# A kept clock that books VectorE's steps longer beside GpSimd, one kind of step per fill, and the last network's transposes in other banks

## The chip, the cores and the metric

The kernel runs on one core of a Trainium2 chip. The metric is the device time of one execution in microseconds, the median of three runs.

## What is computed

Three layers follow one another on 1152 tokens (2 batches of 576) of width 512: attention over a window of 128 with 8 heads and a linear bias; a network of four experts which all run and are weighted by normalised probabilities; and a last network with a squared relu, whose hidden width 2048 the kernel treats as two more experts.

```
x   = window attention(q, k, v)                 # 8 heads of 64
p   = probs / sum(probs)
x   = sum over e of p[e] * (relu(x @ w1[e]) @ w2[e])     # 512 -> 1024 -> 512, e = 0..3
out = square(relu(x @ w_in)) @ w_out                     # 512 -> 2048 -> 512
```

## The kernel before

All matmuls take float32 operands in two rounded parts, high and low, and add three products (high by high, high by low, low by high). The rounding of a weight is two kinds of step: ScalarE copies the tile to its rounded part and GpSimd subtracts for the rest (`rest`, L489).

A planner orders the attention and expert 0 (about the first 143 us). Behind it stands a loop over `items`. An item of one kind is a first matmul group of 384 tokens and one 128-wide tile of hidden units, followed by its second group (`gemm1`, L925, and `gemm2`, L1149). An item of the other kind, a pair (`gemm1_pair`, L1039, and `gemm2_pair`, L1114), computes a two by two block product with seven products instead of eight; its operands are sums: of weight blocks (`w_forms`, made by GpSimd at L345, rounded by ScalarE at L369, rests by GpSimd into `ls`) and of blocks of x (`x_forms`, VectorE at L961, ScalarE at L992). Experts 1 (its second half), 2, 3 and the second half of the last network (e = 5) run as pairs; expert 0, the first half of expert 1 and e = 4 don't. The first pair starts near 226 us, e = 4 runs from 479 to 577, e = 5 behind it. Within a pair three banks `pa`, `pb`, `pc` hold the products: `p1` copies the first one (ScalarE, L1050), `u2` adds it to the second (VectorE, L1054), and the fifth product accumulates on the bank that `u2` has read; `u3` does the same for the seventh. For e = 5 the squared relu of the first block goes by ScalarE (L1068), a VectorE product (L1069) and a copy to `hmem` (L1070). The second group's results gather in banks of kind "y" and VectorE adds them into SBUF (L1164 to L1176).

The weights of the last network come as float64 and are made into float32 from their two 32-bit words, in 32 units (`convert`, L223): a load, ScalarE's `begin` (L268), on VectorE a clamp (L275), a shift (L278) and two joins (L285), then a store from ScalarE's queue (L251). They are read again later by SyncE's queue.

What runs between the matmul groups is set by `fill(share, us, need)`. It moves a kept clock on by the booked length of the matmuls just issued (`clock["now"]`) and then issues background steps: a step of `xbg` (sums of x) on every other call, up to three steps of conversion if `need` is above 0 and credit is there, then weight steps `bg` by quota. The kept clock also holds the booked end of each engine's queue (`spent`); `room` and `by` let a step pass when an engine or an earlier result is near enough, `spare` when VectorE would still be done within `need`. If weights are not ready when an item needs them, `want` issues all that is missing ahead of the item. All engines run their instructions in the order of issue.

The transposed tiles of x for the last network (`to_x2`) come in while expert 3 ends and in the first items of e = 4; they take a bank of kind "work", of which there are three, shared with `hps`. There are five banks of kind "y".

Of the kernel before, what the change touches and what calls it, by code (L numbers as in the profile page):

```python
# [130 lines left out]
def kernel(  # L131
# [91 lines left out]
    def convert():  # L223
# [10 lines left out]
        def load(j, eng):  # L234
            i, h = todo[j]
            src, nk, nf = w_src(*order[i])
            raw[j] = places[j % 2][0]
            m = nk // 2
            eng.dma_start(
                out=raw[j].rearrange("p (k f) t -> p k (f t)", k=m).bitcast(mybir.dt.int64),  # L240
                in_=src[:, h * m:(h + 1) * m, :],
            )
            at["raw", j] = clock["now"] + 6.0

# [13 lines left out]
        def steps(j):  # L258
            a = both[:, j % 2, :]
            ai = a.bitcast(I32)  # L260

            def begin():
                if not (by(at["raw", j]) and by(at.get(("gone", j - 2), 0.0))):
                    return False
                if not room("ACT", 1.2):
                    return False
                hi = raw[j][:, :, 1]
                nc.scalar.activation(out=a, in_=hi.bitcast(F32), func=ACTF.Abs, scale=65536.0)  # L268
                at["a", j] = spent("ACT", 0.7)

            def shift():
                if not (by(at["a", j]) and spare(1.1)):
                    return False
                spent("DVE", 1.1)
                nc.vector.tensor_scalar(  # L275
                    out=a, in0=a, scalar1=8053063680.0, scalar2=2.0, op0=ALU.min, op1=ALU.max
                )
                nc.vector.tensor_scalar(  # L278
                    out=ai, in0=ai, scalar1=3, scalar2=None, op0=ALU.logical_shift_left
                )  # L280

            def join(part, amount, op):
                if not spare(0.8):
                    return False
                nc.vector.scalar_tensor_tensor(  # L285
                    out=ai, in0=raw[j][:, :, part], scalar=amount, in1=ai, op0=op,
                    op1=ALU.bitwise_or,
                )
                at["out", j] = spent("DVE", 0.8) + 0.5

            ops = [
                begin, shift, lambda: join(1, -(1 << 31), ALU.bitwise_and),
                lambda: join(0, 29, ALU.logical_shift_right),
            ]
            if j:
                ops.insert(1, lambda: swap(j - 1))
            if j + 1 == len(todo):
                ops += [lambda: swap(j), lambda: (fxkeep.append(places[0]), fxkeep.append(places[1]),
                                                  free.append(buf))[-1]]
            return ops  # L300
# [17 lines left out]
    def spare(us):  # L318

        now = clock["now"]  # L320
        return clock["force"] or max(clock["DVE"], now) + us <= now + clock["need"]

    def by(end):

        return clock["force"] or end <= clock["now"] + 0.5

    def w_forms(i):
# [14 lines left out]
        def add(o, x, y, op):  # L342
            if not room("POOL"):
                return False
            nc.gpsimd.tensor_tensor(out=t["s"][:, o:o + 2, :], in0=x(), in1=y(), op=op)  # L345
            t["end"] = spent("POOL", 0.75)

# [10 lines left out]
        def part_lo(o, src):  # L358
            if not room("POOL"):
                return False  # L360
            js = slice(o, o + 2)
            rest("POOL", t["la"][0][:, js, :], src, t["ha"][0][:, js, :])
            spent("POOL", 0.75)

        def round_s(o):
            if not (by(t["end"]) and room("ACT", 1.2)):
                return False
            js = slice(o, o + 4)
            nc.scalar.activation(out=t["hs"][0][:, js, :], in_=t["s"][:, js, :], func=ACTF.Copy)  # L369
            t["hs", o] = spent("ACT", 0.6)  # L370

        def done(o):
# [6 lines left out]
            rest("POOL", t["ls"][0][:, js, :], t["s"][:, js, :], t["hs"][0][:, js, :])  # L379
            spent("POOL", 0.75)  # L380
            if o == 6:
# [18 lines left out]
    def w_ops(i):  # L400
# [24 lines left out]
        def lo(o):  # L425
# [3 lines left out]
            rest("POOL", flat(held[0][1])[:, cs], raw[:, cs], flat(held[0][0])[:, cs])  # L429
            spent("POOL", 0.75)  # L430
            if o == 2 * n - 2 * P:
# [519 lines left out]
    def x_forms(ch, eng):  # L951
# [14 lines left out]
        def make(i, name, terms):  # L966
# [12 lines left out]
            def total(k):  # L979
# [4 lines left out]
                else:  # L984
                    z, o = more[k - 1]
                    op(place(i), place(i), f32(z), o)
                end["sum"] = spent("DVE", 0.9)

# [6 lines left out]
            def lo():  # L995
                if not room("DVE"):
                    return False
                op(f[name][1], place(i), f32(f[name][0]))
                spent("DVE", 0.9)

# [26 lines left out]
    def gemm1_pair(e, ch, g):  # L1027
# [29 lines left out]
        def relu(i, j, src, place=None):  # L1057
            hh, hl = (x[:, j * n:(j + 1) * n] for x in h[i])
            spent("DVE", 0.2 + 0.0013 * n, step)
            spent("ACT", 0.1 + 0.0009 * n, step)  # L1060
# [30 lines left out]
        mm(pa, a12, f["b21"], False, True)  # L1091
        relu(0, 0, pa, c22)
        mm(pb, s3, f["t3"], False, False)
        add(u3, pb, p1)
        fill(0.6, step)
        mm(pc, s4, f["b22"], False, True)
# [7 lines left out]
        relu(1, 1, c22)  # L1104
        fill(0.6, step, 1.5 + 1.4 * (2 * n // P))
        return h
# [73 lines left out]

    def to_x2(nt):
        tp = ps_tile("work", [P, KT, P], "xtp")
        for k in range(KT):
            nc.tensor.transpose(
                out=tp[:, k, :], in_=ytile[nt][:, k * P:(k + 1) * P], identity=ident
            )
        ns = slice(nt * P, (nt + 1) * P)
        nc.scalar.activation(out=xh[:, :, ns], in_=tp, func=ACTF.Copy)
        nc.vector.tensor_tensor(out=xl[:, :, ns], in0=tp, in1=f32(xh[:, :, ns]), op=ALU.subtract)  # L1189
# [49 lines left out]

    def run_x2(n=1):  # L1240
        for _ in range(min(n, len(x2todo))):
            to_x2(x2todo.pop(0))

    def flush_one():
# [9 lines left out]
        for tile_ in ys[e, ch]:  # L1254
# [4 lines left out]
            if last:  # L1259
                evac(e, ch, [tile_], f, two)  # L1260
            elif two:
                run_x2()
            i = len(ys[e, ch]) - 1 - tile_[0]
            need = 1.5 + (1.38 - 0.74 * last) * i if two else 3.0 + 0.69 * i
            fill(0.5 if two and last else 1.0, 1.38 if two else 0.69, need)
# [47 lines left out]
    def fill(share, us, need=0.0):  # L1313
# [4 lines left out]
        if xbg and (x_turn[0] % 2 or x_late):  # L1318
            if xbg[0]() is not False:
                xbg.pop(0)  # L1320
        conv_due[0] = min(conv_due[0] + RATE * us, 6.0)
        for _ in range(3):
            if conv and need and conv_due[0] >= 1.0 and conv[0]() is not False:
                conv_due[0] -= 1.0
                conv.pop(0)
        quota["left"] += quota["n"] * share / quota["per"]
        while quota["left"] >= 1.0:
            if not bg_some(1):
# [316 lines left out]
    fxwork, fxbuf, fxkeep, x_late, conv = [], [], [], [], []  # L1645
    conv_due, RATE = [0.0], 0.6

# [7 lines left out]
    xbg = x0_most + x1_most + x0_last + x1_last  # L1655
    xbg.append(lambda: (free.extend(fxbuf), fxbuf.clear()))
    x_turn = [0]

# [14 lines left out]
    for it, (e, ch, f, two) in list(enumerate(items))[N1:]:  # L1673
# [8 lines left out]
        if e >= E and (ch or f):  # L1682
            run_x2()
        quota["n"] = pace(it)
        if two:
            while xbg and (ch or e > E and len(xbg) > x_rest[0]):
                clock["force"] = True
# [69 lines left out]
```

## Time and profile before

| | us |
|---|---|
| median of 3 runs | 687.25 |
| lowest and highest | 686.38, 688.24 |
| the profiled execution | 685.12 |
| its span, first to last instruction | 683.3 |

Busy share of that span: TensorE 97%, VectorE 69%, GpSimd 55%, ScalarE 45%. The granted clock of TensorE was 0.99 over the span. Times in the rows below are microseconds from the span's start. A group names a source line, an engine and the tile written, "<-" the tiles read; a bracket gives the idle time of the engine before the instruction and who ended it.

### The profile page before, as it was taken

Reading aid. Unit: us, or ns where it says so; the run is one execution under the profiler, and the core shown is the slowest. Engines: PE = TensorE matmul, PEld = TensorE weight load, DVE = VectorE, ACT = ScalarE, POOL = GpSimd, SP = SyncE. Lnnn points to the kernel's source line nnn. Section 1 sums busy time; section 2 is a strip of 40 time slices with the busy share of each in tenths; the row PEclk is TensorE's granted clock in tenths of the full one; section 3 lists DMA queues with packets and bytes.
Section 4 is the critical chain, followed back from the end, with each engine's and each line's share of the span. In section 5 each row is a group of like instructions: output and inputs, shape, how many; then the busy total and the mean of one; then the engine's idle time right before and its main releaser. Section 6 shows DMA issues by size and latency. Waiting matters only on the chain.

```text
span 683.3 us, 10748 instructions
## 1 busy us (share of the span) xinstructions
PE 664.7 (97%) x3840; PEld 590.6 (86%) x3840; DVE 472.3 (69%) x958; ACT 308.6 (45%) x745; POOL 378.1 (55%) x459
## 2 busy tenths in 40 slices
PE   8999999999999989999999999999999999899997
PEld 7778888889999878898888989898899899799896
DVE  4798898844768887878878877877458543644453
ACT  5798787623323433434334443433455443423220
POOL 3799995527600954735645644242458974864321
PEclk8999999999999999999999999999999999999999
DMA  8943222013423342443343525343101011000012
GB/s 211 276 110 93 66 78 57 11 63 112 165 80 105 108 155 92 154 129 117 115 151 108 170 78 183 125 154 109 61 2 67 26 62 31 2 0 1 1 63 77
DMA packets 44022, 64.42 MB, mean 94 GB/s; under 512 B 4160, under 2 KB 26176, under 8 KB 43968
## 3 DMA queue, kind: packets, MB, share of 16 engines
q1 hardware_dynamic: 33248, 39.61, 19.3%
q10 hardware_dynamic: 10720, 24.12, 10.5%
q8 instruction: 30, 0.49, 0.3%
q14 instruction: 24, 0.20, 0.1%
HBM read 52.97 MB, written 10.75 MB: 93 GB/s over the span
## 4 chain that ended last, share of the span: by engine, by line
PE 70%; POOL 10%; DVE 9%; issue 6%; ACT 2%; SPq 1%; DMA 1%; POOLq 0%; ACTq 0%
PE yacc L1114 21%; PE hps L1039 20%; PE hps L925 11%; PE yacc L1149 10%; POOL wl L489 4%; PE xps L720 3%; POOL hmem L489 2%; PE tp L848 2%; DVE wconv L285 2%; DVE hmem L1075 2%; DVE y L1168 2%; PE sc L800 1%; POOL wsum L345 1%; DMA rk<-in_kT_dram 1%; DVE c L1054 1%
## 5 line engine op out<-in xcount | busy, mean ns | idle before, releaser
L1114 PE MATMUL yacc<-wh,hmem 128*128 128x512 f32 x504 | 160.8, 391 | 0.0
L489 POOL TENSOR_TENSOR wl<-wraw,wh 128x256 fp32r<-128x256 f32 (+1 forms) x118 | 108.6, 946 | 77.6 <-ACT wh L422 52.9
L1149 PE MATMUL yacc<-wh,hmem 128*128 128x512 f32 x344 | 112.0, 393 | 0.4 <-POOL hmem L489 0.4
L1114 PEld LDWEIGHTS yacc<-wh,hmem 128*128 128x128 f32 x504 | 94.7, 188 | 19.1
L1114 PE MATMUL yacc<-wl,hmem 128*128 128x512 f32 x252 | 98.4, 390 | 0.0
L925 PE MATMUL hps<-xh,wh 128*128 128x384 f32 (+1 forms) x256 | 83.2, 325 | 0.6 <-DVE xl L1189 0.6
L925 PE MATMUL hps<-xh,wl 128*128 128x384 f32 (+1 forms) x256 | 81.6, 319 | 0.0
L925 PE MATMUL hps<-xl,wh 128*128 128x384 f32 (+1 forms) x256 | 81.5, 318 | 0.0
L1149 PEld LDWEIGHTS yacc<-wh,hmem 128*128 128x128 f32 x344 | 64.5, 188 | 13.9 <-POOL hmem L489 0.8
L1149 PE MATMUL yacc<-wl,hmem 128*128 128x512 f32 x172 | 67.3, 391 | 0.0
L489 POOL TENSOR_TENSOR ls<-wsum,hs 128x256 fp32r<-128x256 f32 x56 | 48.2, 884 | 31.2 <-ACT hs L369 30.5
L1050 ACT ACTIVATE p<-hps 128x256 f32<-128x256 f32 (+1 forms) x56 | 22.7, 408 | 77.7 <-PE hps L1039 63.8
L285 DVE SCALAR_TENSOR_TENSOR wconv<-wraw,wconv 128x512 int32<-128x512 int32 x64 | 56.4, 881 | 1.8
L345 POOL TENSOR_TENSOR wsum<-wraw 128x256 f32<-128x256 f32 x28 | 24.1, 862 | 56.6 <-PE hps L925 35.5
L1114 PEld LDWEIGHTS yacc<-wl,hmem 128*128 128x128 f32 x252 | 47.4, 188 | 8.8
L836 POOL TENSOR_SCALAR ts<-ts,st 128x256 f32<-128x256 f32 (+2 forms) x80 | 40.6, 521 | 25.7 <-DVE st L831 12.1
L1074 ACT ACTIVATE hmem<-c 128x256 fp32r<-128x256 f32 (+1 forms) x60 | 26.1, 445 | 56.7 <-DVE c L1054 55.9
L489 POOL TENSOR_TENSOR hmem<-c,hmem 128x256 fp32r<-128x256 f32 (+1 forms) x32 | 27.1, 856 | 43.3 <-ACT hmem L1070 29.0
L925 PEld LDWEIGHTS hps<-xh,wh 128*128 128x128 f32 x256 | 48.2, 188 | 2.0 <-DVE xl L1189 1.0
L925 PEld LDWEIGHTS hps<-xl,wh 128*128 128x128 f32 x256 | 48.3, 189 | 0.7 <-issue 0.2
L489 POOL TENSOR_TENSOR hmem<-r,hmem 128x384 fp32r<-128x384 f32 x24 | 26.0, 1086 | 40.2 <-ACT hmem L1136 40.1
L925 PEld LDWEIGHTS hps<-xh,wl 128*128 128x128 f32 x256 | 48.2, 188 | 0.0
(141 smaller groups left out, 1670.6 us busy)
## 6 DMA issues: line engine op xcount, KB each, us to landing
wraw<-in_w_dram SPq DMA_DIRECT2D x32, 512.0 KB, 4.6
w<-wconv ACTq DMA_DIRECT2D x32, 256.0 KB, 2.4
wraw<-in_w_out_dram ACTq DMA_DIRECT2D x16, 512.0 KB, 3.9
wraw<-w SPq DMA_DIRECT2D x16, 512.0 KB, 4.0
wraw<-in_w_in_dram ACTq DMA_DIRECT2D x14, 512.0 KB, 3.8
rq<-in_qT_dram SPq DMA_DIRECT2D x8, 256.0 KB, 7.1
out_dram<-y SPq DMA_DIRECT2D x8, 256.0 KB, 2.0
rk<-in_kT_dram SPq DMA_DIRECT2D x8, 192.0 KB, 5.9
```

The source lines that it names most:

```text
L285: nc.vector.scalar_tensor_tensor(out=ai, in0=raw[j][:, :, part], scalar=amount, in1=ai, op0=op, op1=ALU.bitwise_or,)
L345: nc.gpsimd.tensor_tensor(out=t["s"][:, o:o + 2, :], in0=x(), in1=y(), op=op)
L489: e.tensor_tensor(out=out, in0=in0, in1=f32(in1), op=ALU.subtract)
L720: nc.tensor.matmul(out=xps[:, :, o0:o0 + w], lhsT=l_, rhs=r_, start=(i == 0 and l_ is wh_ and r_ is hi), stop=(i == len(mm) - 1 and l_ is ...
L836: nc.gpsimd.tensor_scalar(out=ts[0:n, g, :], in0=ts[0:n, g, :], scalar1=st[0:n, 2, g:g + 1], scalar2=1.0, op0=ALU.mult, op1=ALU.mult,)
L848: nc.tensor.transpose(out=tp[0:cn, g, k * n:(k + 1) * n], in_=s["ts"].tile[0:n, g, c0:c0 + cn], identity=ident[0:n, 0:n],)
L925: nc.tensor.matmul(out=ps, lhsT=l_[:, k, cs], rhs=r_[:, k, cols], start=(k == 0 and r_ is xh and l_ is wh and not second), stop=(k == KT - ...
L1039: nc.tensor.matmul(out=ps, lhsT=a[l_][:, k, :], rhs=b[r_][:, k, :], start=start and k == 0 and l_ == r_, stop=stop and k == 1 and l_ == 1, ...
L1050: nc.scalar.activation(out=out, in_=x, func=ACTF.Copy)
L1074: nc.scalar.activation(out=hh, in_=src, func=ACTF.Relu)
L1114: nc.tensor.matmul(out=y, lhsT=l_[:, ns], rhs=r_[:, fo, :], start=(first and fo == 0 and j == 0), stop=(last and fo == FTQ - 1 and j == 2),)
L1149: nc.tensor.matmul(out=y, lhsT=l_[:, ns], rhs=r_[:, fo, :], start=(first and j == 0), stop=(last and j == 2),)
```

## The change

The kept clock: a VectorE step asked for by `spare` is booked at 1.6 times its length while GpSimd's booked end lies ahead, at 1.1 times else, and `spare` books it itself. Clamp and shift become two steps at 0.45 (one at 1.1 before), a join costs 0.65 (0.8). GpSimd's steps cost 0.85 (0.75), the sums of x 0.2 + 0.003 n (0.9). `by` takes how early a step may pass, and for two of them it is 0. The windows `need` behind a pair's first group and its output tiles start from 0.8 (1.5). `fill` issues no weight step in a call that issued a conversion step; the credit of conversion is capped at 12 (6). In the last network the first relu of a pair is issued behind `u3`, and the transposes of e = 4 take banks of kind "y" and are booked. The sums of x that a first pair needs are forced ahead of it for every expert.

```diff
-            at["raw", j] = clock["now"] + 6.0
+            at["raw", j] = clock["now"] + 7.0
...
-            def shift():
-                if not (by(at["a", j]) and spare(1.1)):
+            def clamp():
+                if not (by(at["a", j], 0.0) and spare(0.45)):
                     return False
-                spent("DVE", 1.1)
                 nc.vector.tensor_scalar(
                     out=a, in0=a, scalar1=8053063680.0, scalar2=2.0, op0=ALU.min, op1=ALU.max
                 )
+
+            def shift():
+                if not spare(0.45):
+                    return False
                 nc.vector.tensor_scalar(
                     out=ai, in0=ai, scalar1=3, scalar2=None, op0=ALU.logical_shift_left
                 )
             def join(part, amount, op):
-                if not spare(0.8):
+                if not spare(0.65):
                     return False
...
-                at["out", j] = spent("DVE", 0.8) + 0.5
+                at["out", j] = clock["DVE"] + 0.5
...
     def spare(us):
         now = clock["now"]
-        return clock["force"] or max(clock["DVE"], now) + us <= now + clock["need"]
-    def by(end):
-        return clock["force"] or end <= clock["now"] + 0.5
+        us *= 1.6 if clock["POOL"] > now + 0.2 else 1.1
+        if not clock["force"] and max(clock["DVE"], now) + us > now + clock["need"]:
+            return False
+        return spent("DVE", us)
+    def by(end, early=0.5):
+        return clock["force"] or end <= clock["now"] + early
...
         def round_s(o):
-            if not (by(t["end"]) and room("ACT", 1.2)):
+            if not (by(t["end"], 0.0) and room("ACT", 1.2)):
...
     def gemm1_pair(e, ch, g):
...
         mm(pa, a12, f["b21"], False, True)
-        relu(0, 0, pa, c22)
+        if e < E:
+            relu(0, 0, pa)
         mm(pb, s3, f["t3"], False, False)
         add(u3, pb, p1)
+        if e >= E:
+            relu(0, 0, pa, c22)
...
-        fill(0.6, step, 1.5 + 1.4 * (2 * n // P))
+        fill(0.6, step, 0.8 + 1.4 * (2 * n // P))
...
-    def to_x2(nt):
-        tp = ps_tile("work", [P, KT, P], "xtp")
+    def to_x2(nt, kind):
+        tp = ps_tile(kind, [P, KT, P], "xtp")
...
+        spent("ACT", 0.6)
+        spent("DVE", 0.7)
...
-            need = 1.5 + (1.38 - 0.74 * last) * i if two else 3.0 + 0.69 * i
+            need = 0.8 + (1.38 - 0.74 * last) * i if two else 3.0 + 0.69 * i
...
-        conv_due[0] = min(conv_due[0] + RATE * us, 6.0)
+        conv_due[0] = min(conv_due[0] + 0.6 * us, 12.0)
+        given = False
         for _ in range(3):
             if conv and need and conv_due[0] >= 1.0 and conv[0]() is not False:
                 conv_due[0] -= 1.0
                 conv.pop(0)
+                given = True
         quota["left"] += quota["n"] * share / quota["per"]
-        while quota["left"] >= 1.0:
+        while quota["left"] >= 1.0 and not given:
...
+    x_rest = [len(x1_last) + 1]
...
         if e >= E and (ch or f):
-            run_x2()
+            run_x2("y")
         quota["n"] = pace(it)
         if two:
-            while xbg and (ch or e > E and len(xbg) > x_rest[0]):
+            while xbg and (ch or len(xbg) > x_rest[0]):
```

## Rows read from the trace of the kernel before

**Rows 1.** Busy us and (x count) of PE, PEld, DVE, ACT, POOL by stage; PEclk, DMA.
```profile
220.00:300.00 80.00, 74.19 (x435) 66.55 (x434) 66.92 (x107) 32.83 (x72) 49.35 (x56) 1.00 0.38 126
300.00:478.00 178.00, 177.59 (x1022) 159.72 (x1021) 141.45 (x240) 68.06 (x146) 81.74 (x95) 1.00 0.40 131
478.00:577.00 99.00, 98.03 (x510) 89.20 (x509) 53.70 (x69) 46.87 (x92) 65.38 (x70) 1.00 0.11 38
```

**Rows 2.** Waits of TensorE, 143 to 684: us in total, times, longest us.
```profile
PE hps L1039 <- DVE u L1054: 7.5, 7, 3.1
PE hps L925 <- DVE xl L1189: 0.6, 1, 0.6
PE yacc L1149 <- POOL hmem L489: 0.4, 1, 0.4
PE hps L1039 <- ACT p L1050: 0.4, 1, 0.4
```

**Rows 3.** Timeline of TensorE: start, us, engine, line, operation, idle before it.
```profile
231.35 0.39 PE L1039 MATMUL hps<-xh,hs 128*128 128x256 f32 x1 [1.58 <-DVE u L1054]
...
239.81 0.28 PE L1039 MATMUL hps<-xh,ha 128*128 128x256 f32 x1
...
246.25 0.38 PE L1039 MATMUL hps<-xh,hs 128*128 128x256 f32 x1 [3.05 <-DVE u L1054]
...
295.33 0.39 PE L1039 MATMUL hps<-xh,hs 128*128 128x256 f32 x1 [0.19 <-DVE u L1054]
...
485.02 0.44 PE L925 MATMUL hps<-xh,wh 128*128 128x384 f32 x1 [0.56 <-DVE xl L1189]
...
582.56 0.38 PE L1039 MATMUL hps<-hm,ha 128*128 128x256 f32 x1 [1.71 <-DVE u L1054]
```

**Rows 4.** Timeline of VectorE, 239 to 246.
```profile
239.73 0.96 DVE L275 TENSOR_SCALAR wconv<-wconv 128x512 f32<-128x512 f32 x1
...
243.31 1.24 DVE L285 SCALAR_TENSOR_TENSOR wconv<-wraw,wconv 128x512 int32<-128x512 int32 x1
...
244.47 1.40 DVE L1168 SCALAR_TENSOR_TENSOR y<-yacc,pt,y 128x512 f32<-128x512 f32 x2
...
245.79 0.41 DVE L1054 TENSOR_TENSOR u<-hps,p 128x256 f32<-128x256 f32 x1
```

**Rows 5.** Conversion lines on VectorE: ns min/median/max, first and last start us.
```profile
L275 DVE TENSOR_SCALAR wconv<-wconv x32: 409/421/961, 192.8 to 478.8; 128x512 f32<-128x512 f32 x32
...
L278 DVE TENSOR_SCALAR wconv<-wconv x32: 426/429/973, 193.2 to 479.2; 128x512 int32<-128x512 int32 x32
...
L285 DVE SCALAR_TENSOR_TENSOR wconv<-wraw,wconv x64: 679/694/1240, 193.7 to 483.3; 128x512 int32<-128x512 int32 x64
```

**Rows 6.** Timeline of ScalarE and its DMA queue, 267 to 269.
```profile
267.41 0.33 ACTq L251 DMA_DIRECT2D w<-wconv  x1
...
268.32 0.77 ACT L1050 ACTIVATE p<-hps 128x320 f32<-128x320 f32 x2 [4.03 <-DVE y L1168]
```

**Rows 7.** Timeline of GpSimd, 227 to 276, the steps that end a form.
```profile
227.95 4.30 POOL L489 TENSOR_TENSOR ls<-wsum,hs 128x256 fp32r<-128x256 f32 x4
...
242.25 3.56 POOL L489 TENSOR_TENSOR ls<-wsum,hs 128x256 fp32r<-128x256 f32 x4
...
274.13 1.68 POOL L489 TENSOR_TENSOR ls<-wsum,hs 128x256 fp32r<-128x256 f32 x2 [2.96 <-ACT hs L369]
```

**Rows 8.** Timeline of VectorE near 480, the last evacuation of expert 3.
```profile
479.58 0.74 DVE L1168 SCALAR_TENSOR_TENSOR y<-yacc,pt,y 128x512 f32<-128x512 f32 x1
```

**Rows 9.** Timeline of ScalarE, 580 to 582.
```profile
580.82 0.63 ACT L369 ACTIVATE hs<-wsum 128x512 fp32r<-128x512 f32 x1 [0.77 <-POOL wsum L345]
581.36 0.37 ACT L1068 ACTIVATE c<-hps 128x256 f32<-128x256 f32 x1
```

**Rows 10.** Timeline of VectorE, 581 to 583.
```profile
581.75 0.42 DVE L1069 TENSOR_TENSOR c<-hps,c 128x256 f32<-128x256 f32 x1 [3.25 <-ACT c L1068]
582.10 0.41 DVE L1054 TENSOR_TENSOR u<-hps,p 128x256 f32<-128x256 f32 x1
```

**Rows 11.** Groups of VectorE by line, 478 to 577: busy us, mean ns, idle before.
```profile
L961 DVE TENSOR_TENSOR fxwork<-fxwork,xl 128x512 f32<-128x512 f32 (+1 forms) x12 | 12.9, 1072 | 0.3
```

More of the change, by code (lines that the diff above doesn't have):

```diff
@@ L288, in join @@
                 )
-                at["out", j] = spent("DVE", 0.8) + 0.5
+                at["out", j] = clock["DVE"] + 0.5
             ops = [
-                begin, shift, lambda: join(1, -(1 << 31), ALU.bitwise_and),
+                begin, clamp, shift, lambda: join(1, -(1 << 31), ALU.bitwise_and),
                 lambda: join(0, 29, ALU.logical_shift_right),
@@ L345, in add @@
             nc.gpsimd.tensor_tensor(out=t["s"][:, o:o + 2, :], in0=x(), in1=y(), op=op)
-            t["end"] = spent("POOL", 0.75)
+            t["end"] = spent("POOL", 0.85)
         def s(o):
@@ L362, in part_lo @@
             rest("POOL", t["la"][0][:, js, :], src, t["ha"][0][:, js, :])
-            spent("POOL", 0.75)
+            spent("POOL", 0.85)
         def round_s(o):
-            if not (by(t["end"]) and room("ACT", 1.2)):
+            if not (by(t["end"], 0.0) and room("ACT", 1.2)):
                 return False
@@ L379, in done @@
             rest("POOL", t["ls"][0][:, js, :], t["s"][:, js, :], t["hs"][0][:, js, :])
-            spent("POOL", 0.75)
+            spent("POOL", 0.85)
             if o == 6:
@@ L429, in lo @@
             rest("POOL", flat(held[0][1])[:, cs], raw[:, cs], flat(held[0][0])[:, cs])
-            spent("POOL", 0.75)
+            spent("POOL", 0.85)
             if o == 2 * n - 2 * P:
@@ L986, in total @@
                     op(place(i), place(i), f32(z), o)
-                end["sum"] = spent("DVE", 0.9)
+                end["sum"] = spent("DVE", 0.2 + 0.003 * n)
             def hi():
@@ L998, in lo @@
                 op(f[name][1], place(i), f32(f[name][0]))
-                spent("DVE", 0.9)
+                spent("DVE", 0.2 + 0.003 * n)
             return [lambda k=k: total(k) for k in range(1 + len(more))] + [hi, lo]
@@ L1058, in relu @@
             hh, hl = (x[:, j * n:(j + 1) * n] for x in h[i])
-            spent("DVE", 0.2 + 0.0013 * n, step)
+            spent("DVE", 0.25 + 0.0015 * n, step)
             spent("ACT", 0.1 + 0.0009 * n, step)
@@ L1238, with run_x2 @@
     x2todo = []
-    def run_x2(n=1):
-        for _ in range(min(n, len(x2todo))):
-            to_x2(x2todo.pop(0))
+    def run_x2(kind):
+        if x2todo:
+            to_x2(x2todo.pop(0), kind)
     def flush_one():
@@ L1261, in flush_one @@
             elif two:
-                run_x2()
+                run_x2("work")
             i = len(ys[e, ch]) - 1 - tile_[0]
-            need = 1.5 + (1.38 - 0.74 * last) * i if two else 3.0 + 0.69 * i
+            need = 0.8 + (1.38 - 0.74 * last) * i if two else 3.0 + 0.69 * i
             fill(0.5 if two and last else 1.0, 1.38 if two else 0.69, need)
@@ L1645 @@
     fxwork, fxbuf, fxkeep, x_late, conv = [], [], [], [], []
-    conv_due, RATE = [0.0], 0.6
+    conv_due = [0.0]
     def fx_room():
@@ L1682 @@
         if e >= E and (ch or f):
-            run_x2()
+            run_x2("y")
         quota["n"] = pace(it)
         if two:
-            while xbg and (ch or e > E and len(xbg) > x_rest[0]):
+            while xbg and (ch or len(xbg) > x_rest[0]):
                 clock["force"] = True
```

## Prediction

> **What bounds the kernel now.** I read the busy time by stage first. TensorE is busy for 74.19 of the 80 us between 220 and 300, for 177.59 of 178 between 300 and 478, for 98.03 of 99 up to 577, and it holds its upper clock level (2.4 GHz, granted clock 1.00) in all of these [rows 1]. So the bound is TensorE's own matmul stream, and no edit here removes a matmul. What can be won is TensorE's idle time behind 143 us; the first 143 us come from the planner, which the diff does not touch. The table of TensorE's waits gives that sum: 7.5 us on the add `u` of VectorE (L1054), 0.6 on `xl` (L1189), 0.4 on GpSimd's `hmem` and 0.4 on ScalarE's copy `p`, together 8.9 us [rows 2]. That is the ceiling of the gain, 1.3% of the span.
>
> Then the timeline, for where they are [rows 3]: 1.58 us at 231.35, 3.05 at 246.25, 0.19 at 295.33, 0.56 at 485.02 and 1.71 at 582.56. The lower half of the chain is read from VectorE: from 239.73 on it works on conversion (a clamp of 0.96 us, a join of 1.24) and evacuations (two in 1.40), and `u` begins only at 245.79 [rows 4]. The matmul at 246.25 accumulates on the bank which `u` reads, so it waits for exactly that backlog. The same steps take 0.42, 0.43 and 0.69 us in the median and 0.96, 0.97 and 1.24 at most [rows 5]; the long join at 243.31 lies beside GpSimd's four `ls` steps from 242.25 on [rows 7]. The kernel's kept clock books 1.1 for the first two and 0.8 for each join wherever they fall: 2.7 for a unit that can take 4.4 (0.96 + 0.97 + twice 1.24). So it issues more conversion than fits.
>
> **Part 1, the kept clock and the windows.** Clamp and shift become separate steps at 0.45, a join costs 0.65, all times 1.6 while the clock holds GpSimd busy and 1.1 else. A unit is then booked at 3.52 beside GpSimd and 2.42 alone; the error beside GpSimd falls from 1.7 us (4.4 - 2.7) to 0.9. The window `need` ends 0.7 us earlier in the fills ahead of the next item (1.5 becomes 0.8), which covers most of that 0.9. What waited for it is the 7.5 us on `u` less the 1.7 at 582.56, and the 0.4 on `p`: 6.2 of the 8.9. The wait on `p` is one of this kind too: ScalarE's queue held the store of a converted half (issue at 267.41) until the join had ended, and the copies queued behind it began at 268.32 after 4.03 us of idle time [rows 6]; the store's due time now hangs on the corrected clock. I take all 6.2 back; the bounds are 0 and 6.2. No VectorE work is added: the two steps are the same two instructions.
>
> **Part 2, one kind of step per fill.** A fill that issued a conversion step issues no weight step. Conversion runs only in fills with a window: the last of five in a pair's first matmul group and the four or five behind the output tiles. So GpSimd's work moves into the four inner fills, where it is paid as longer VectorE adds from SBUF, off the path. The place where it can hurt is the first pair of expert 1: its second item starts at 239.81 [rows 3], and the prepared forms for it end with four `ls` steps, 227.95 to 232.25 [rows 7]. The lead is 7.5 us, and all eleven GpSimd steps have to come out of some 19 fills, about half of which may now go to conversion. If the last four come late they stand in front of the item: 4.30 us at most, 0 at least. The lead is nearer to enough than to none; I take 1.0. For the second form, `ls` ends at 275.81 [rows 7] and its item begins near 292 (the row at 295.33 is the 25th of its 42 matmuls, which the code books at 5.3 us together), so there the lead is 16 us, and I take 0.
>
> Conversion itself gets slower: 6 closures a unit instead of 5, at an unchanged 0.6 per us. 32 units are 192 closures; less the 12 of initial credit they need 300 us from 192.8 [rows 5], so it ends at 493 at the earliest instead of 483. VectorE is busy for only 53.70 of 99 us between 478 and 577 [rows 1], so there I book 0.
>
> **Part 3, sums of x.** They are booked at 0.97 and 1.16 instead of 0.9, and they are guarded by `room`, so a few may be left when the first pair starts; the new test `x_rest` then forces them in front of it. The list puts the first pair's own last sum behind most of the other chunk's. I take 0: TensorE's first wait behind that start, at 231.35, was on `u` and none was on a sum [rows 2, 3]; the other end is three steps of 1.07 us [rows 11], 3.2.
>
> **Part 4, transposes in y's banks.** In the last network the transposed tiles shared three banks with the hidden products; at 485.02 TensorE waited 0.56 us for `xl` to free one [rows 3]. The five banks of y are free by then: the last of the five evacuations ahead of them ends at 479.58 + 0.74 = 480.32 [rows 8], and they free the banks in the order in which the transposes take them. The transposes now queue on TensorE behind those evacuations, and all matmuls behind them; cost 0 as long as VectorE keeps up, 0.74 for each evacuation by which it falls behind. I take the 0.56 back.
>
> **Part 5, the first relu later.** At 582.56 TensorE has waited 1.71 us for the add `u3`. `u3` (582.10 to 582.51) stood behind the product at 581.75, which had waited 3.25 us for ScalarE's L1068 [rows 10]; that began at 581.36, right behind a rounding that had waited 0.77 us for GpSimd [rows 9]. In the change `u3` comes ahead of that product, so it needs only its own matmuls, which ended before TensorE fell idle at 580.85 (582.56 - 1.71), and roundings wait for GpSimd's booked end. ScalarE's order is as before; the product and what follows it come one add (0.41 us) later, against a whole item of slack before the second matmul group reads them. I take 1.7 back; the other end is 0.
>
> **The sum.** 6.2 + 0.56 + 1.7 - 1.0 = 7.5 us. The profiled execution took 685.12 us; it becomes 677.6. The median of the runs, 687.25, lies 2.13 above that execution, so the forecast is 680.
>
> **A rule that speaks against it.** Clamp and shift read and write SBUF alone, and their longest run is 0.54 us over the median [rows 5]. The Trainium skill (SBUF, section "Who interferes with whom") says that such an instruction, in the mode that takes both of VectorE's ports, and one of GpSimd exclude each other, that issue order decides which of them waits, and that the loser waits for the other's whole instruction. By that a fixed factor is the wrong form: a step that loses would wait up to a GpSimd step (4.30 / 4 = 1.08 us [rows 7]), more than the 0.27 that the factor adds to a clamp. The rows agree only in part, since 0.54 is half a GpSimd step. What hangs on it is the first rival.
>
> **The rivals.** *The waits change owner.* A clamp beside GpSimd is booked at 0.72 and can take 0.96, and forms and sums of x pile up at the first pair. Then the waits of 220 to 478 stay in other hands (late `ls`, forced sums), the 6.2 us are not won, and only parts 4 and 5 remain: 687.25 - 2.3 = 685, or 686 with 1.0 for the forms. For it: VectorE is busy 66.92 of 80 us there and GpSimd 49.35 [rows 1], so there is little free room. Against it: the 0.7 us of window alone is more than waits like the 0.19 at 295.33 need.
>
> *Weights starve (slower).* In 300 to 478 GpSimd issues 95 steps in 81.74 us, 0.86 each [rows 1]; at 11.8 us an item (the code's figure) that is 6.3 per item. In the four inner fills the kept clock lets through about (4.3 + 1.2 + 0.4) / 0.85 = 7: the four fills' booked time, the 1.2 us that `room` allows ahead, half a step over, at the new 0.85 a step. That holds as long as none of it waits for a rounding; if stops leave it 1.5 steps short per item, 21 items from 226 to 478 are 27 us late, less the 16 us of lead: 11 us on TensorE, 691. It decides from 16 / (21 x 0.86) = 0.9 steps per item. Against it: a fill in which conversion has no window or no credit falls to the weights.
>
> *Conversion ends too late (slower).* Before, 160 closures less 6 of credit were 257 us, and the last join began at 483.3 [rows 5], 34 us behind that pace. Losing as much again it ends near 527; if the 26 sums for the last pairs wait for it, at 1.07 us each [rows 11] they end near 555, against a first pair near 577. Past that, each us stands in front of that pair: the point is 22 us more, and 32 us more gives 680 + 10 = 690.
>
> **How the numbers follow.** Forecast (676 to 684): 0.60. Waits change owner (684 to 687.5): 0.20. Weights starve: 0.12. Conversion too late: 0.08. The floor is 687.25 - 8.9 = 678.3, less the 0.9 by which the fastest run lies under the median and some 2 us of spread more, 675.5. From 675.5 to 689 no more than the two slower cases is left out; the forecast's own range, 676 to 684, holds part 2 at 3.4 more than taken. A difference of 0.3% (2.1 us) is about what a measurement of this kernel can tell; below 685.2 lie the forecast and a fifth of the second case: 0.64; within, 0.16; above 689.3, 0.20.
>
> **What would show it.** Right: no TensorE wait on `u` over 1 us between 220 and 300, TensorE busy there 78 us or more, `u3` ahead of the product at the first pair of the last half, no wait for `xl` near 485, the last join near 500. Wrong: TensorE idle ahead of a pair's first matmul with GpSimd in `ls` or `wl`, or at the first pair with VectorE in `fxwork`; a last join past 530.

## The result, and the profile after

The changed kernel took 674.5 us (median of 4 runs, 674.17 to 675.13) beside 686.82 for the kernel before (four runs now; the three of the table above had 687.25): a ratio of 0.9819, interval 0.9801 to 0.9837, 12.3 us faster. The forecast was 680.0 with a range of 675.5 to 689.0, so the direction was right and the gain was larger than the range allowed. The profiled execution took 674.21 us, 10.9 less than that of before.

Busy time by stage in the changed kernel, columns as in [rows 1]:

```profile
220.00:300.00 80.00, 79.58 (x474) 72.59 (x474) 58.49 (x101) 33.45 (x74) 49.12 (x60) 1.00 0.36 117
300.00:478.00 178.00, 177.22 (x1023) 159.62 (x1023) 127.37 (x229) 67.13 (x144) 75.45 (x92) 1.00 0.35 116
478.00:577.00 99.00, 99.00 (x524) 90.53 (x522) 73.88 (x96) 51.05 (x101) 75.67 (x74) 1.00 0.23 75
```

TensorE fills 79.58 of the first 80 us (74.19 before). VectorE's work has moved: it is busy 8 us less from 220 to 300, 14 less from 300 to 478 and 20 more from 478 to 577. (The stretches are the same in time, and the changed kernel is some 2 to 10 us further in them.) TensorE's waits from 143 us on, as in [rows 2], are one line:

```profile
PE hps L1045 <- DVE u L1060: 1.2, 4, 0.4
```

The 8.9 us of [rows 2] are 1.2. The waits on `xl`, `hmem` and `p` are gone, and no wait on `u` is longer than 0.42. At the place of the 3.05 us wait [rows 3, 4] VectorE now holds one conversion unit, which ends before the evacuations; its `u` starts at 240.81 and TensorE does not wait for it:

```profile
235.31 0.42 DVE L274 TENSOR_SCALAR wconv<-wconv 128x512 f32<-128x512 f32 x1
235.77 0.85 DVE L281 TENSOR_SCALAR wconv<-wconv 128x512 int32<-128x512 int32 x1
236.65 2.26 DVE L288 SCALAR_TENSOR_TENSOR wconv<-wraw,wconv 128x512 int32<-128x512 int32 x2
238.83 2.06 DVE L1177 SCALAR_TENSOR_TENSOR y<-yacc,pt,y 128x512 f32<-128x512 f32 x3
240.81 0.41 DVE L1060 TENSOR_TENSOR u<-hps,p 128x256 f32<-128x256 f32 x1
```

The steps themselves did not become shorter. The view of [rows 5], of the changed kernel:

```profile
L274 DVE TENSOR_SCALAR wconv<-wconv x32: 415/424/1239, 192.7 to 531.6; 128x512 f32<-128x512 f32 x32
...
L288 DVE SCALAR_TENSOR_TENSOR wconv<-wraw,wconv x64: 675/694/1503, 193.6 to 535.9; 128x512 int32<-128x512 int32 x64
```

The medians are those of before, and the longest clamp and join are longer (1239 and 1503 ns against 961 and 1240). What changed is where they lie; the last join begins at 535.9. GpSimd's end of the first form, as in [rows 7]:

```profile
229.98 2.82 POOL L495 TENSOR_TENSOR ls<-wsum,hs 128x256 fp32r<-128x256 f32 x4 [1.02 <-ACT hs L375]
```

It ends at 232.80, 5.6 us ahead of its item (238.44).

### The profile page after: what moved, and what is told of

It reads as the page before. It is cut to its first block, busy times and chain, and to the rows that moved or that the text cites. A ratio compares the mean times of both kernels' runs of the same rounds, so it can differ in the third digit from the quotient of the medians.

```text
span 672.4 us, 10765 instructions
## 1 busy us (share of the span) xinstructions
PE 661.8 (98%) x3840; PEld 590.8 (88%) x3840; DVE 465.0 (69%) x958; ACT 307.7 (46%) x745; POOL 376.4 (56%) x459
## 4 chain that ended last, share of the span: by engine, by line
PE 88%; DVE 5%; POOL 3%; ACT 2%; issue 1%; DMA 1%; SPq 0%; POOLq 0%; ACTq 0%; DVEq 0%
PE yacc L1123 23%; PE hps L1045 21%; PE hps L931 17%; PE yacc L1158 17%; PE xps L726 3%; PE tp L854 2%; PE sc L806 2%; POOL wl L495 1%; DVE y L1177 1%; DVE wconv L288 1%; PE sc L799 1%; DVE hmem L1081 1%; PE hps L1571 1%; POOL ts L842 1%; DVE c L1060 1%
## 5 line engine op out<-in xcount | busy, mean ns | idle before, releaser
L495 POOL TENSOR_TENSOR wl<-wraw,wh 128x256 fp32r<-128x256 f32 (+1 forms) x118 | 110.0, 956 | 92.7 <-ACT wh L428 69.2
L1060 DVE TENSOR_TENSOR u<-hps,p 128x256 f32<-128x256 f32 (+1 forms) x56 | 25.5, 455 | 50.9 <-PE hps L1045 50.8
L288 DVE SCALAR_TENSOR_TENSOR wconv<-wraw,wconv 128x512 int32<-128x512 int32 x64 | 58.1, 907 | 1.5
L495 POOL TENSOR_TENSOR ls<-wsum,hs 128x256 fp32r<-128x256 f32 x56 | 46.2, 850 | 16.7 <-ACT hs L375 16.2
L351 POOL TENSOR_TENSOR wsum<-wraw 128x256 f32<-128x256 f32 x28 | 22.5, 803 | 49.6 <-PE hps L931 36.1
```

What stands on the lines that cost most here:

```text
L288: nc.vector.scalar_tensor_tensor(out=ai, in0=raw[j][:, :, part], scalar=amount, in1=ai, op0=op, op1=ALU.bitwise_or,)
L495: e.tensor_tensor(out=out, in0=in0, in1=f32(in1), op=ALU.subtract)
L1060: nc.vector.tensor_tensor(out=out, in0=x, in1=y, op=ALU.add)
```

## The experiments

Each run stood beside the kernel before on the same chip. First the two edits of the last network's start, together and alone, added to the kernel before.

```diff
-        relu(0, 0, pa, c22)
+        if e < E:
+            relu(0, 0, pa)
         mm(pb, s3, f["t3"], False, False)
         add(u3, pb, p1)
+        if e >= E:
+            relu(0, 0, pa, c22)
...
-    def to_x2(nt):
-        tp = ps_tile("work", [P, KT, P], "xtp")
+    def to_x2(nt, kind):
+        tp = ps_tile(kind, [P, KT, P], "xtp")
...
-            run_x2()
+            run_x2("y")
```

> The kernel before with two parts of the change alone: the transposes of the last network in y's banks, and its first relu behind u3. If each wait costs its idle time and some 0.27 us more (the matmul ahead of it is drawn 0.16 us longer than its pace, the one behind it runs 0.1 us slower), the waits of 0.56 and 1.71 us are worth 2.8 us: 684.0 against 686.8. If the idle time alone is the price, 2.3: 684.5. If the waits only move to another owner, 686.8.

> The kernel before with the transposes in y's banks alone. 0.8 us less by the trace (0.56 and the restart): 686.1 against 686.9. If the share of the time that varies from run to run lies at the transposes, 684.3.

> The kernel before with the first relu of the last network behind u3 alone. 2.0 us less by the trace (1.71 and the restart): 684.9 against 686.9. If the share that varies from run to run lies at this wait, 683.2.

Both together: 683.26 us, ratio 0.9948 (0.9933 to 0.9963), 3.6 less than before. Banks alone: 685.96, 0.9987 (0.9975 to 1.0), about 0.9, with an interval that reaches to no difference. The relu alone: 685.05, 0.9978 (0.9966 to 0.9989), about 1.5. Each edit removes its wait: with the banks the one at 485 us is gone, with the relu the one at 582 us. The starts of the same matmuls tell their worth more closely than the medians. From the first matmul of e = 4 (479.23) to the one at 489.99 TensorE takes 10.76 us in the kernel before, and 9.72 with the banks alone and with both. From the one at 576.97 to the one at 589.99 it takes 13.02, with the relu alone 11.12 and with both 11.09. So in the kernel before the two are worth 1.0 and 1.9 us, for 0.56 and 1.71 of idle time shown; the medians also differ by what varies between executions, above all the clock behind another wait, which comes further down. TensorE's waits with both edits:

```profile
PE hps L1039 <- DVE u L1054: 5.7, 6, 3.0
PE hps L1039 <- ACT p L1050: 0.5, 2, 0.4
PE yacc L1152 <- POOL hmem L489: 0.4, 1, 0.4
```

The other side of the same cut is the changed kernel without both edits, so with the schedule alone.

```diff
-        if e < E:
-            relu(0, 0, pa)
+        relu(0, 0, pa, c22)
...
-        if e >= E:
-            relu(0, 0, pa, c22)
...
-            run_x2("y")
+            run_x2("work")
```

> The changed kernel with both edits of the last network's start taken back (its transposed tiles behind y again, its first relu ahead of the sum u3 again), so that only the new clock, the narrower window, the single kind per fill and the moved sums of x are left. If the parts add up, the 3.2 to 3.6 us that the two edits brought to the kernel before come back on top: 674.2 + 3.4 = 677.6 us. If their places hardly matter once fewer steps are handed out (the relu alone cost 0.6 us there, the wait at 485 us was 0.56), about 674.2 + 0.6 + 0.6 = 675.4 us, with a wait of some 0.5 us for xl near 475 us and none over 1 us near 572.

675.1 us, 0.983 (0.9813 to 0.9846), so the second expectation came, without its wait for `xl`: 0.6 above the changed kernel and 11.3 below the runs of before beside it (686.36). TensorE's waits in it:

```profile
PE hps L1045 <- DVE u L1060: 1.0, 3, 0.4
PE hps L1045 <- ACT p L1056: 0.2, 1, 0.2
```

The parts do not add up, and the reason is in the order on ScalarE and VectorE. ScalarE's timeline of the kernel before, then VectorE's, ahead of the `xl` that ends the wait at 485.02:

```profile
483.14 0.62 ACT L422 ACTIVATE wh<-wraw 128x512 fp32r<-128x512 f32 x1
483.66 0.58 ACT L1188 ACTIVATE xh<-xtp 128x512 fp32r<-128x512 f32 x1
```
```profile
482.59 1.41 DVE L285 SCALAR_TENSOR_TENSOR wconv<-wraw,wconv 128x512 int32<-128x512 int32 x2
484.27 0.69 DVE L1189 TENSOR_TENSOR xl<-xtp,xh 128x512 fp32r<-128x512 f32 x1 [0.28 <-ACT xh L1188]
```

`xl` waited for ScalarE's copy `xh`, which stood behind the rounding of a weight, `wh`. VectorE had been free for 0.28 us by then; until 484.00 it worked on two joins, which would have held `xl` next. In the run with the schedule alone no rounding stands right ahead of `xh`, and the next join comes behind `xl`:

```profile
476.30 0.58 ACT L1196 ACTIVATE xh<-xtp 128x512 fp32r<-128x512 f32 x1
```
```profile
476.92 0.69 DVE L1197 TENSOR_TENSOR xl<-xtp,xh 128x512 fp32r<-128x512 f32 x1 [0.29 <-ACT xh L1196]
...
478.29 0.68 DVE L288 SCALAR_TENSOR_TENSOR wconv<-wraw,wconv 128x512 int32<-128x512 int32 x1
```

So the wait for `xl` was made by a rounding, and behind it by conversion. At the first pair of the last half ScalarE's timeline has the relu's copy (L1074, L1068 before) right behind a copy `p` and ready when TensorE is, where a rounding of `hs` that waited for GpSimd stood in [rows 9], and another one (579.42, 0.25 us of waiting) ahead of it:

```profile
570.51 0.38 ACT L1056 ACTIVATE p<-hps 128x256 f32<-128x256 f32 x1 [0.23 <-PE hps L1045]
571.17 0.38 ACT L1074 ACTIVATE c<-hps 128x256 f32<-128x256 f32 x1 [0.28 <-PE hps L1045]
```

The changed kernel with the place of the relu alone taken back says the same:

> The changed kernel with the first relu of the last network where it was, ahead of u3. If the place of the relu is what removed the wait of 1.71 us, 676.5 with a TensorE wait on u of over 1 us at the first pair of e = 5. If the later due time of ScalarE's roundings is enough, 674.5 and no such wait.

675.13 us, 0.9836 (0.9813 to 0.986), and the wait of 1.7 us did not come back.

Then the parts of the schedule, each taken out of the changed kernel.

```diff
-        while quota["left"] >= 1.0 and not given:
+        while quota["left"] >= 1.0:
```

> The changed kernel, but a fill that issued a conversion step may issue weight steps too. If booking and window do the work, within 1 us of 674.5, with TensorE's waits on u under 2 us in all. If keeping GpSimd away from VectorE's steps does it, the joins get longer (mean above 0.95 us in place of 0.91), waits on u of 1 us and more come back, and the time is 678 or more.

677.74 us, 0.9867 (0.9851 to 0.9884): weight steps beside conversion in one fill cost 3.2 us. The joins are not longer for it (mean 863 ns against 907), so that part of the expectation was wrong. TensorE's wait on `u` grew to 3.4 us in 8 pieces. The longest stands at 573.75. VectorE's timeline there:

```profile
570.85 1.24 DVE L967 TENSOR_TENSOR fxwork<-xh 128x640 f32<-128x640 f32 x1
572.13 1.23 DVE L967 TENSOR_TENSOR fxwork<-fxwork,xl 128x640 f32<-128x640 f32 x1
573.29 0.41 DVE L1060 TENSOR_TENSOR u<-hps,p 128x256 f32<-128x256 f32 x1
```

Two sums of x stand in front of the pair's `u`. GpSimd makes sums of weights beside them:

```profile
571.49 1.19 POOL L351 TENSOR_TENSOR wsum<-wsum,wraw 128x256 f32<-128x256 f32 x1
```

In the changed kernel GpSimd has four `wl` steps there (568.66 to 572.08), and no sum of x stands in VectorE's way. This is read from the longest wait; the other seven, of 0.21 to 0.57 us, were not traced back.

```diff
-        us *= 1.6 if clock["POOL"] > now + 0.2 else 1.1
+        us *= 1.1
```

> The changed kernel, but a conversion step is booked at 1.1 times its length wherever it falls. If booking beside GpSimd is what removed the waits on u, about half of them come back (3 us): 677.5 to 678. If the shorter window alone is enough, 674.5 to 675.

676.45 us, 0.9846 (0.9832 to 0.9861), between the two values that were expected: the longer booking beside GpSimd is worth 2.0 us. Waits on `u` are 3.1 us, with 1.10 at 242.53 and 1.36 at 572.73, the latter again behind the two sums.

```diff
-        fill(0.6, step, 0.8 + 1.4 * (2 * n // P))
+        fill(0.6, step, 1.5 + 1.4 * (2 * n // P))
...
-            need = 0.8 + (1.38 - 0.74 * last) * i if two else 3.0 + 0.69 * i
+            need = 1.5 + (1.38 - 0.74 * last) * i if two else 3.0 + 0.69 * i
```

> The changed kernel with the window of before (1.5 in place of 0.8). If the 0.7 us of window is what keeps u on time, waits on u of 0.3 to 1 us come back at most pair items that begin behind evacuations, ten or so: 677 to 681. If the booking is enough, 674.5 to 675.5.

> The changed kernel with the wide window (1.5 in place of 0.8) once more, beside the changed kernel on one chip. If the narrow window costs three waits of 0.24 to 0.28 us and what comes with them (0.5 us each), 1.5 us under the changed kernel: 672.8 to 673.0.

> The changed kernel once more, to be compared with the wide window on one chip: 674.5.

With the old windows 672.81 us, 0.9794 (0.978 to 0.9809), below both values that were expected; again, on one chip with the changed kernel, 672.68 (672.5 to 672.97) beside 674.18 (674.04 to 674.49). The narrower window costs 1.5 us. This version beats both kernels. Its only wait is the one at 231 us:

```profile
PE hps L1045 <- DVE u L1060: 0.4, 1, 0.4
```

VectorE's timeline of the changed kernel at one of the three waits that are missing here (311.73, 0.28 us) shows how a smaller window can hurt. A unit whose clamp ran at 295.13 got its shift and both joins only here, in front of four evacuations and `u`:

```profile
305.81 0.41 DVE L281 TENSOR_SCALAR wconv<-wconv 128x512 int32<-128x512 int32 x1
306.26 2.38 DVE L288 SCALAR_TENSOR_TENSOR wconv<-wraw,wconv 128x512 int32<-128x512 int32 x2
308.57 2.71 DVE L1177 SCALAR_TENSOR_TENSOR y<-yacc,pt,y 128x512 f32<-128x512 f32 x4
311.20 0.47 DVE L1060 TENSOR_TENSOR u<-hps,p 128x320 f32<-128x320 f32 x1
```

With the wider window the clamp and the shift lie there, 0.82 and 0.84 us, and `u` starts at 309.96. That the smaller window held the shift back is read from the rows. The run without the factor points to the booking beside it: its only waits are at 231, 243, 266 and 573 us, so these three are missing there too, and the shift follows its clamp:

```profile
297.42 0.43 DVE L281 TENSOR_SCALAR wconv<-wconv 128x512 int32<-128x512 int32 x1
```

So by these rows the 2.0 us of the factor are a balance: it removes the waits of 1.10 and 1.36 us and has a part in these three, together with the narrow window.

Last, the part of the gain that no wait in [rows 2] shows. The kernel before again, first in ten executions, then twice in a single one with its trace:

> The kernel before once more, for a second profile of it. The first profiled execution took 685.12 us, 1.8 under the median of the runs since (686.9), and the two parts tried alone saved 1.9 us against that execution but 3.6 against the median. If the first profile caught a rare short execution, this one is near 687 and shows some 1.8 us more of TensorE waits, and they lie between 478 and 600, where those two parts act. If the profile itself runs shorter than the timed runs, this one is near 685 again.

> The kernel before, unchanged, looked at once more. If the 2 us by which its profiled executions (684.5 and 685.1) lay under its median (686.8) are TensorE's clock behind the 3 us wait at 246 us, then an execution near the median shows a granted clock near 0.5 for some us right behind that wait, and one near 685 shows 1.00 there. If the 2 us come from elsewhere (the start, attention), an execution near 687 has the same 1.00 there and is longer in another stretch.

> The same look a second time: an execution over 686 us with a granted clock near 0.5 behind 246 us, or one near 685 with 1.00, if the clock makes the difference; any other pairing speaks against it.

The median was 686.36 us (684.5 to 687.75), ratio 0.9996 (0.9983 to 1.0009), and the profiled execution took 684.5: it looked as if the profile itself ran shorter. The two single ones took 685.99 and 688.02, so it does not. So there are four profiled executions of one program. Busy time and granted clock (the third number from the end) behind the longest wait, first in that of 685.12 us:

```profile
246.60:252.00 5.40, 5.40 (x34) 4.79 (x33) 3.96 (x7) 2.75 (x6) 2.48 (x4) 1.00 0.10 36
```

In that of 685.99 us:

```profile
246.60:252.00 5.40, 5.40 (x29) 4.95 (x29) 3.07 (x6) 2.31 (x6) 1.60 (x3) 0.80 0.02 3
```

In that of 688.02 us:

```profile
246.60:252.00 5.40, 5.40 (x22) 5.11 (x23) 2.65 (x6) 1.76 (x4) 0.92 (x2) 0.50 0.00 0
```

In the fourth, of 684.5 us, the wait was 2.47 us and the clock 1.00. In the longest one TensorE ran this stretch at the lower level, 1.2 GHz. TensorE's timeline in it, the end of the wait, the next matmuls, and the sixth matmul of the second group, which serves as a mark:

```profile
246.59 0.58 PE L1039 MATMUL hps<-xh,hs 128*128 128x256 f32 x1 [3.04 <-DVE u L1054]
246.97 0.41 PE L1039 MATMUL hps<-xl,hs 128*128 128x256 f32 x1
247.18 0.41 PE L1039 MATMUL hps<-xh,ls 128*128 128x256 f32 x1
...
252.62 0.62 PE L1114 MATMUL yacc<-wh,hmem 128*128 128x512 f32 x2
```

From the end of the wait to this matmul it takes 6.03 us (252.62 - 246.59). In the execution of 685.12 us it takes 3.48 (246.25 to 249.73), in that of 684.5 it takes 3.45, in that of 685.99 it takes 4.67. The clock cost 2.55 and 1.19 us, and with the start of these pairs (the wait at 231 us ends at 231.35, 230.99 and 231.69) this is the whole difference: 2.55 + 0.34 = 2.89 of 2.90, and 1.19 - 0.36 = 0.83 of 0.87. That of 684.5 waited 0.58 less and took 0.62 less than that of 685.12. Three more traces hold the same wait untouched, those with the banks, with the relu and with both. It is 3.04 us in each; the clock behind it is 0.52, 0.50 and 0.72, and the way to the mark takes 5.89, 6.14 and 4.91 us, so 2.41, 2.66 and 1.43 more than 3.48. Of six executions with the wait at its full length five lost clock. So what sets these executions apart is the clock behind the wait that the change removes; that it makes the median's distance from the first profile too is worked out from these traces, the other executions having none. The Trainium skill (TensorE: Matmul & The Clock Gate, Part 1) says that an idle TensorE falls back to half its clock, and that one kernel differs from run to run in how long it runs slowly at its start. Five of the six executions agree with the first, and the clocks of 1.00, 0.80 and 0.50 show such a difference behind a wait in the middle of a kernel.

The opposite test puts a late `u` into the changed kernel at the same place, by four additions in front of it and, in a second run, by eight (`range(8)`):

```diff
+        if (e, ch, g) == (1, 0, 3):
+            for _ in range(4):
+                nc.vector.tensor_tensor(out=c22, in0=pb, in1=p1, op=ALU.add)
         add(u2, pb, p1)
```

> The changed kernel with four more additions of 0.41 us on VectorE in front of one u, that of the second pair item near 240 (their result is overwritten later). There u ends just in time for TensorE. A wait of about 1.5 us comes back at that matmul. If a wait costs its own length and little more, 674.5 + 1.7 = 676.2, and the granted clock behind it stays at 1.00.

> The same with eight additions: a wait of about 3.1 us, as long as the one of the kernel before at 246.25. If idle time and restart are all, 674.5 + 3.4 = 677.9 and the clock stays at 1.00. If TensorE's clock falls behind a wait of this length in most executions, as it did in the profiled runs of the two parts tried alone and not in that of the kernel before, 1.5 to 2.5 us more: 679.5 to 680.5 in the median, with 3 us between runs, and the profiled run shows 0.5 to 0.75 of the clock for some 5 us behind the wait.

With four additions 676.18 us, 0.9843 (0.983 to 0.9856); with eight 679.09, 0.9886 (0.9872 to 0.9899). TensorE's timeline with four:

```profile
243.18 0.39 PE L1045 MATMUL hps<-xh,hs 128*128 128x256 f32 x1 [1.51 <-DVE u L1060]
```

With eight, the end of the wait and the mark:

```profile
245.12 0.39 PE L1045 MATMUL hps<-xh,hs 128*128 128x256 f32 x1 [3.35 <-DVE u L1060]
...
250.06 0.62 PE L1126 MATMUL yacc<-wh,hmem 128*128 128x512 f32 x2
```

With eight, the stretch behind the wait, columns as in [rows 1]:

```profile
246.00:249.00 3.00, 3.00 (x15) 2.90 (x15) 1.64 (x5) 0.42 (x1) 0.00 (x0) 0.52 0.00 0
```

The wait of 1.51 us costs 1.7 (2.0 beside the changed kernel on the same chip, 674.18) and leaves the pace of the matmuls behind it unchanged (128x256 every 0.12 us). The one of 3.35 us takes the clock to 0.52, some 0.9 us behind its end: from its end to the same mark it is 4.94 us, 1.46 more than 3.48. The four executions lie within 0.63 us, and not 3 us apart as expected. TensorE's waits from 143 us on were 3.4 us more than in the changed kernel, in one piece more; 674.21 + 3.4 + 0.26 (a piece, below) + 1.46 is 679.3, and that execution took 679.47. Without the clock it would be 677.9.

## Why the prediction was wrong

**The bound and the first step** were right. TensorE's stream sets the time, and of 8.9 us of waits 7.7 went where the sum had 7.5. That these two agree is in part luck: the sum took all waits on `u` and `p` back and lost 1.0 to late forms, while 1.2 on `u` stayed, nothing was lost to forms, and the 0.4 on `hmem`, which the sum left, went too.

**"That is the ceiling of the gain"** was wrong, and it carried the range. A wait costs more than the idle time shown. On TensorE's timeline of the kernel before the last matmul ahead of the first wait and the first two behind it are

```profile
229.49 0.28 PE L1039 MATMUL hps<-xh,la 128*128 128x256 f32 x1
231.35 0.39 PE L1039 MATMUL hps<-xh,hs 128*128 128x256 f32 x1 [1.58 <-DVE u L1054]
231.58 0.28 PE L1039 MATMUL hps<-xl,hs 128*128 128x256 f32 x1
```

At the pace of this stretch, one every 0.12 us, the last of them would have started at 229.73. It started 1.85 us later, for 1.58 of idle: 0.16 because a matmul is drawn 0.28 long and the next would have started inside it, and 0.1 because the first one behind the wait delays its follower. At 0.26 a wait the experiments close: without the rule of one kind, 2.2 more idle and 4 waits more are 3.2 (measured 3.2); with the old window, 0.8 less and 3 waits less are 1.6 (measured 1.5 and 1.7). Between the two profiles lie 10.9 us: 7.7 of idle, some 1.6 for six waits fewer, and the rest, 1.6, in starts of the kernel before that come up to 0.4 us late with little or no idle shown (0.15 of it ahead of 143 us).

**"The median lies 2.13 above that execution, so the forecast is 680"** was the step that moved the centre. The distance was taken for a constant of measuring. As worked out above it is the clock behind the wait of 3.05 us, which the same sum removes. The changed kernel's profiled execution lies 0.3 under its median. Without that term the forecast was 677.6 plus 0.3, still 3.4 above 674.5: 3.2 for the starts and 0.2 for the idle time. So of the 12.3 us some 7.7 are idle time, 3.2 starts and 1.4 the clock (1.7 by which the median of before lay above its profile, less 0.3).

**Part 1** was booked at 6.2 us with two causes, and one of them had the wrong sign: taken out alone, the factor is worth 2.0 us (676.45 without it), and the narrower window costs 1.5. **Part 2** was a cost of 1.0 and is worth 3.2; the form came 5.6 us ahead of its item. The lead was judged from the steps that the rule takes away, and not from what it spares VectorE. **Part 3** at 0 was right: TensorE's wait at the first pair is 0.42 us, at 231.48. Its ground was not: that the wait at 231.35 was "on `u`" names the last instruction, and in the kernel before two sums of x (227.20, 2.63 us) and a join stood ahead of that `u`. At the first pair of the last network sums stand in front too, at 1.36 us, when the rule or the factor is missing. **Parts 4 and 5** were booked at 0.56 and 1.7. They are worth 1.0 and 1.9 in the kernel before, and 0.6 together behind the schedule, which removes both waits by itself. The error was to give each wait to the edit that names its last instruction, when a late rounding stood behind both, and conversion behind the first.

**The rivals.** *Waits change owner* did not happen, though the sums at 572 us without the rule are this mechanism. *Weights starve*: no wait of TensorE on weights is shown. *Conversion too late*: it ended near 537, later than this rival's 527, and the text took a join past 530 as a sign of error. The sign came and cost nothing, as VectorE had the room and the first pair's sums did not wait for it. The last join was not near 500, as the prediction had it for being right. The rest of those signs came as told: TensorE 79.58 us busy, no wait near 485, `u3` ahead of the product:

```profile
571.59 0.42 DVE L1060 TENSOR_TENSOR u<-hps,p 128x256 f32<-128x256 f32 x1 [1.66 <-PE hps L1045]
571.93 0.41 DVE L1075 TENSOR_TENSOR c<-hps,c 128x256 f32<-128x256 f32 x1
```

**The rule on the ports** is borne out, and "half a GpSimd step", which spoke against it, was a misreading. The longest clamp of the changed kernel took 0.82 us over the median. It began inside a GpSimd rest that had 0.95 us still to run. VectorE's timeline, then GpSimd's:

```profile
531.65 1.24 DVE L274 TENSOR_SCALAR wconv<-wconv 128x512 f32<-128x512 f32 x1
```
```profile
530.99 1.61 POOL L495 TENSOR_TENSOR hmem<-r,hmem 128x384 fp32r<-128x384 f32 x1
```

The clamp of [rows 4], at 239.73, is 0.54 over the median, and this step of GpSimd had 0.67 left then:

```profile
239.22 1.18 POOL L489 TENSOR_TENSOR la<-wraw,ha 128x256 fp32r<-128x256 f32 x1
```

It goes like this through both traces. Of the 128 clamps and shifts 45 begin inside a GpSimd step with more than 0.2 us of it left. 44 of them are longer by what is left of that step, less 0.14 us. The one exception began 0.01 us behind its step and lost nothing, and the other 83 take 0.41 to 0.43 us. The Trainium skill (SBUF, "Who interferes with whom") says that whoever issues first holds the ports for its whole instruction while the other is blocked, and these rows agree but for the one exception. What is lost is thus not a share of a step but what is left of it. A factor of 1.6 underbooks the clamp of 1.24 us (0.72), and it sufficed here because that clamp lay where TensorE waited for nothing of VectorE.

What stays open: how the 11.3 us of the schedule divide between its bookings, beyond the three parts taken out one at a time, since these depend on each other.

## What to carry to other kernels

Price a wait on the bounding engine by the starts of the work around it, not by the idle time shown, and ask of every long one what the clock does behind it, in several executions: the distance between a profile and its median can belong to the very wait that is to be removed. Where steps are handed out by a kept clock, a wait belongs to whatever filled the queue, so edits aimed at its last instruction and edits of the schedule are not to be added. Test each constant of such a schedule alone: here two that were meant to do the same had opposite signs when each was taken out alone.

## What the runs showed of the hardware

A TensorE wait of about 3.05 us left the granted clock at 1.00 in one execution, 0.80 and 0.50 in two others of the same program, at a cost of 0, 1.19 and 2.55 us behind the wait; 1.51 and 2.47 us left the pace alone, 3.35 lowered it. At 0.50 a 128x256 matmul starts every 0.21 us (246.97, 247.18), at 1.00 every 0.12. A clamp or shift of conversion that begins while a GpSimd step runs waits for what is left of it, less 0.14 us, in 44 of 45 cases of two traces. VectorE's sums of x and GpSimd's sums of weights lengthen each other where they meet: in the run without the rule of one kind a 128x640 sum took 1.23 to 1.24 us beside a `wsum` step of 1.19. In the changed kernel such a sum takes 0.81 where GpSimd does nothing, and a `wsum` step 0.74 where VectorE makes no sum of x. VectorE's timeline, then GpSimd's:

```profile
233.00 0.81 DVE L967 TENSOR_TENSOR fxwork<-fxwork,xl 128x640 f32<-128x640 f32 x1
```
```profile
241.69 0.74 POOL L351 TENSOR_TENSOR wsum<-wraw,wsum 128x256 f32<-128x256 f32 x1
```

In the execution with four additions the granted clock reads 0.95 in every stretch at the upper level, while the matmuls start 0.12 us apart as at 1.00: there the figure alone does not mean a slower pace.
